# Biased attention and channel mix: float64 weights converted by bits, their range tested on a second read, low parts made by TensorE

## The chip, the core and the metric

The kernel runs on one core of one Trainium2 chip. The metric is the device time of one execution in microseconds. The engines are called as the profile calls them: PE (TensorE, matmuls) with PEld (its weight loads), DVE (VectorE), ACT (ScalarE), POOL (GpSimd) and SP (SyncE, which issues the DMAs).

## What is computed

An attention with a distance bias over a sliding window of 96 keys and 8 global keys, and behind it a channel mix with a gate. Shapes: q, k, v are (4, 8, 768, 64) in float32; w_k is (512, 1024), w_v (1024, 512) and w_r (512, 512), all three in float64.

```python
keep = (pos_k < 8) | ((rel >= 0) & (rel < 96))
scores = where(keep, q @ k.T / 8 - slope[h] * dist, -1e9)
x = softmax(scores) @ v                     # heads side by side: (4, 768, 512)
xk = mu_k * x + (1 - mu_k) * x_prev         # x_prev: the row before in the sequence
xr = mu_r * x + (1 - mu_r) * x_prev
k2 = relu(xk @ w_k) ** 2
out = sigmoid(xr @ w_r) * (k2 @ w_v)
```

## The kernel before

The sequence is cut into 24 tiles of 128 rows (6 for each of 4 batches). For each tile the attention makes scores on PE (`scores`, line 302), adds the bias on DVE (L323), takes the exponential on ACT (L324), scales by the reciprocal of the sum on POOL or ACT (L332 to L337), transposes on PE (L349), copies on ACT (L351) and multiplies with v on PE (L368). Tiles 0 to 7 multiply q and k as whole float32 (L314, L315); later tiles use split operands.

Two tiles make a chunk of 256 rows, and there are 12 chunks. `ffn` (L451) mixes each chunk with the row before it (`mix`, DVE L395) and splits it into a high and a low part (`xk_hi` by an ACT cast, `xk_lo` by a DVE subtraction). `channel_mix` (L400) multiplies them with split weights, three matmuls for each product (high x high, high x low, low x high: `three`, L403). In a chunk there are four blocks `kp` for xk @ w_k, each followed by Relu on ACT (L431), the square on DVE (L432), the high part on ACT (L433) and the low part on DVE (L434); then two blocks `z` for the gate, and two blocks `vps` for the product with w_v, each followed by the multiplication on DVE (L448) and the store. The three PSUM tiles of `ps_f` (tag "f") are shared by kp, z and vps.

The weights come as float64 and are converted in ten steps of 1 MB: w_k has steps 0 to 3, w_r has 4 and 5, w_v has 6 to 9. `weight_load` reads the two 32-bit words of each number (`low`, `top`). `weight_begin` (L161) builds a float32 `wa` from them: ACT takes an absolute value with a scale (L172 or L175), which clamps what is out of float32's range together with a POOL operation for w_k (L173) or a DVE operation for the others (L176); then DVE puts exponent, sign and fraction together with three bit operations (L177 to L179), and ACT casts the high part (L181). `weight_end` (L184) makes the low part by a DVE subtraction (L187).

A loop over tiles (L475) interleaves attention and channel mix by a budget, and the tables `W_LOADS` and `W_BEGUN` say when weight steps are loaded and begun. The order in which each engine then works is made by a scheduler at build time, from its own costs; each engine runs its list in order. At the end a flag `wide_i` is read by all five engines (L630), which then branch over a general path (`wide`) for sizes outside the tables (L631). The flag depends on the two sizes alone, and DVE writes it in the first 10 us.

Of the kernel before, what the change touches and what calls it, by code (L numbers as in the profile page):

```python
# [9 lines left out]
F32 = mybir.dt.float32  # L10
F32R = mybir.dt.float32r
# [30 lines left out]
def tile_biased_attention_channel_mix(ctx: ExitStack, tc: tile.TileContext, qT, kT, v, n_sizes, mu_kr, w_k, w_v, w_r, q_rows, k_rows, v_rows, slopes, out):  # L42
# [102 lines left out]
    pool.tensor_scalar(mus1, mus, -1.0, 1.0, op0=ALU.mult, op1=ALU.add)  # L145

    w_steps = [(name, src, j) for name, src, pairs in (("k", w_k, 4), ("r", w_r, 2), ("v", w_v, 4)) for j in range(pairs)]
    w_raw, w_live = {}, {}

    def weight_load(i):  # L150


        name, src, j = w_steps[i]
        raw = w_raw[i] = const.tile([128, 1024, 2], I32, tag=f"w{i}", name=f"w64_{i}")
        if name == "k":
            ins = nc.sync.dma_start(raw.rearrange("p n w -> p (n w)"), src[j * 128 : (j + 1) * 128, :])
        else:
            ins = nc.sync.dma_start(raw.rearrange("p (k n) w -> p k (n w)", k=2), src[j * 256 : (j + 1) * 256, :].rearrange("(k p) m -> p k m", p=128))
        tc.keep_in_program_order(ins)

    def weight_begin(i):  # L161


        name, src, j = w_steps[i]
        raw = w_raw.pop(i)
        a = p4k.tile([128, 1024], I32, tag="t4k", name=f"wa_{i}")
        low, top = raw[:, :, 0], raw[:, :, 1]

        if name == "k":
            act.activation(a.bitcast(F32), top.bitcast(F32), AF.Abs, scale=2.0**111)  # L172
            pool.tensor_scalar(a.bitcast(F32), a.bitcast(F32), 2.0**-112, 2.0**-111, op0=ALU.mult, op1=ALU.mult)  # L173
        else:
            act.activation(a.bitcast(F32), top.bitcast(F32), AF.Abs, scale=2.0**16)  # L175
            vec.tensor_scalar(a.bitcast(F32), a.bitcast(F32), 2.0, HUGE, op0=ALU.max, op1=ALU.min)  # L176
        vec.tensor_scalar(a, a, 3, 0x7FFFFFF8, op0=ALU.logical_shift_left, op1=ALU.bitwise_and)  # L177
        vec.scalar_tensor_tensor(a, top, -0x80000000, a, op0=ALU.bitwise_and, op1=ALU.bitwise_or)
        vec.scalar_tensor_tensor(a, low, 29, a, op0=ALU.logical_shift_right, op1=ALU.bitwise_or)  # L179
        both = const.tile([128, 2, 1024], F32R, tag=f"w{i}", name=f"w{name}{j}")  # L180
        act.copy(both[:, 0, :], a.bitcast(F32))  # L181
        w_live[i] = a, both

    def weight_end(i):  # L184
# [117 lines left out]
    def scores(n, hp):  # L302
        t = n % NT
        s = state[n]
        c0 = 0 if t else OWN
        w = W - c0
        p = pat if t else pat0
        ps = ps_s.tile([128, 512], F32, name=f"s_{n}_{hp}", tag="s")
        for u in range(2):
            h = 2 * hp + u  # L310
            o = ps[:, u * 256 : u * 256 + w]
            if n < NATIVE:
                if t:
# [12 lines left out]
        if hp % 2 == 0:  # L326
            return
        h0, nh = 2 * hp - 2, 4
        r = s_pool.tile([128, nh], F32, name=f"r_{n}_{hp}", tag="r", bufs=8)
        vec.tensor_scalar(r, s["sum"][:, h0 : h0 + nh], 1.0e-9, None, op0=ALU.add)  # L330
        vec.reciprocal(r, r)  # L331
        for u in range(nh):  # L332
            e = s["e"][h0 + u]
            if n < 6 and u < 2:
                act.mul(e[:, :w], e[:, :w], r[:, u : u + 1])
            else:
                pool.tensor_scalar(e[:, :w], e[:, :w], r[:, u : u + 1], 1.0, op0=ALU.mult, op1=ALU.mult)  # L337
# [59 lines left out]
        vec.tensor_sub(lo, tmp, hi)  # L397
        return hi, lo

    def channel_mix(xk, xr, out_rows, f_pool, f2_pool, ps_f):  # L400
        kkh, kkl = (part(f_pool, f"kk_{p}", 8) for p in ("hi", "lo"))

        def three(o, sh, sl, mh, ml, first, last):  # L403
            pe.matmul(o, sh, mh, start=first, stop=False)  # L404
            pe.matmul(o, sh, ml, start=False, stop=False)  # L405
            pe.matmul(o, sl, mh, start=False, stop=last)  # L406

        def z_of(i):
            z = ps_f.tile([128, 512], F32, name="z", tag="f")
            c = slice(i * 128, (i + 1) * 128)  # L410
            for k in range(4):
                three(z, xr[0][:, k, c], xr[1][:, k, c], *wts["r", k], k == 0, k == 3)
                yield
            sig = f2_pool.tile([128, 512], F32, name="sig", tag="f2")
            sigs.append((z, sig))

        sigs = []
        for fp in range(4):
            weights_need(4)
            ps = ps_f.tile([128, 512], F32, name="kp", tag="f")  # L420
# [12 lines left out]
            act.copy(kkh[:, 2 * fp : 2 * fp + 2, :], kk)  # L433
            vec.tensor_sub(kkl[:, 2 * fp : 2 * fp + 2, :], kk, kkh[:, 2 * fp : 2 * fp + 2, :])  # L434
        weights_need(6)
        for i in range(2):
            yield from z_of(i)
        for z, sig in sigs:
            act.activation(sig, z, AF.Sigmoid)
        for i in range(2):  # L440
            c = slice(i * 128, (i + 1) * 128)
            vp = ps_f.tile([128, 512], F32, name="vps", tag="f")
            sig = sigs[i][1]
            for f in range(8):
# [12 lines left out]

    LAG = 3
# [218 lines left out]
```

## Time and profile before

| what | value |
|---|---|
| time, median of 3 runs | 511.14 us (510.61 to 512.39) |
| the profiled execution | 510.47 us, of which the span of the trace is 508.6 us |
| PE busy in the span | 490.6 us (96%) |
| DVE, ACT, POOL busy | 345.8, 338.0 and 215.7 us |
| moved by DMA | 49.46 MB, mean 97 GB/s |

The span runs from the first to the last instruction of the program; the execution's own time is 1.9 us longer. A busy share says how much of the span an engine had an instruction in work, and the granted clock says at which of its two levels TensorE ran (1.00 is 2.4 GHz, 0.50 is 1.2 GHz). The shares are means over stretches that differ, so the stretches are read apart below.

### The profile page before, as it was taken

How to read it: one execution, taken by the hardware profiler on the slowest of the kernel's cores; microseconds unless marked ns; L12 is line 12 of the kernel's file. 1: busy time of each engine (PE TensorE's matmuls, PEld its weight loads, DVE VectorE, ACT ScalarE, POOL GpSimd, SP SyncE). 2: the span in 40 equal slices, each digit the busy share in tenths (PEclk: the TensorE clock that was granted, in tenths of full speed). 3: DMA queues.
4: the chain of work that ended last, by engine and by line, in shares of the span. 5: the costliest groups of instructions: out<-in, count | busy, mean ns of one | idle time of the engine just before them, and what ended most of it. 6: DMA issues, size and time to landing. Idle time of an engine off the chain costs nothing. (4 is left out here: it accounts for less than half of the span.)

```text
span 508.6 us, 10113 instructions
## 1 busy us (share of the span) xinstructions
PE 490.6 (96%) x3562; PEld 434.5 (85%) x3562; DVE 345.8 (68%) x826; ACT 338.0 (66%) x826; POOL 215.7 (42%) x359
## 2 busy tenths in 40 slices
PE   7949998999999999999999999999999999999996
PEld 4838987998898898898898898898898898898984
DVE  6799989755468777757768767757768765535321
ACT  4999999757448759567668578567668578654230
POOL 7432216243348546427538436527538535203000
PEclk9987999999999999999999999999999999999999
DMA  8998611513733333433323433333433221100101
GB/s 236 320 245 233 214 43 39 121 43 79 172 92 79 104 101 81 107 97 80 105 84 79 105 101 79 104 101 79 106 82 80 64 60 39 41 1 2 41 2 46
DMA packets 21353, 49.46 MB, mean 97 GB/s; under 512 B 5008, under 2 KB 6032, under 8 KB 20784
## 3 DMA queue, kind: packets, MB, share of 16 engines
q1 hardware_dynamic: 21152, 48.74, 35.4%
q8 instruction: 30, 0.49, 0.4%
q14 instruction: 27, 0.22, 0.1%
q10 hardware_dynamic: 144, 0.00, 0.0%
HBM read 42.44 MB, written 6.29 MB: 96 GB/s over the span
## 5 line engine op out<-in xcount | busy, mean ns | idle before, releaser
L337 POOL TENSOR_SCALAR e<-e,r 128x232 f32<-128x232 f32 (+1 forms) x168 | 82.4, 507 | 162.1 <-DVE r L331 134.1
L404 PE MATMUL kp<-xk_hi,wk 128*128 128x256 f32 x384 | 108.4, 283 | 0.4 <-ACT xk_hi L396 0.4
L405 PE MATMUL kp<-xk_lo,wk 128*128 128x256 f32 x384 | 107.3, 280 | 0.0
L406 PE MATMUL kp<-xk_hi,wk 128*128 128x256 f32 x384 | 107.2, 279 | 0.0
L324 ACT ACTIVATE e<-e,nmax 128x232 f32<-128x232 f32 (+1 forms) x192 | 89.6, 470 | 22.9 <-DVE nmax L323 22.3
L323 DVE CUSTOM_DVE_ANT_0 e<-s,pat 128x232 f32<-128x232 f32 (+1 forms) x192 | 64.5, 373 | 24.8 <-PE s L318 14.3
L404 PE MATMUL vps<-wv,kk_hi 128*128 128x512 f32 x192 | 75.2, 394 | 0.0
L406 PE MATMUL vps<-wv,kk_lo 128*128 128x512 f32 x192 | 75.2, 392 | 0.0
L405 PE MATMUL vps<-wv,kk_hi 128*128 128x512 f32 x192 | 75.2, 391 | 0.0
L404 PEld LDWEIGHTS kp<-xk_hi,wk 128*128 128x128 f32 x384 | 72.0, 188 | 1.4 <-ACT xk_hi L396 0.6
L405 PEld LDWEIGHTS kp<-xk_lo,wk 128*128 128x128 f32 x384 | 72.1, 188 | 0.4
L406 PEld LDWEIGHTS kp<-xk_hi,wk 128*128 128x128 f32 x384 | 72.1, 188 | 0.0
L432 DVE TENSOR_TENSOR kk<-kp,kk 128x512 f32<-128x512 f32 x48 | 33.1, 689 | 46.5 <-ACT kk L431 46.3
L351 ACT COPY et<-t 128x256 f32<-128x256 f32 (+1 forms) x176 | 56.2, 372 | 8.6 <-PE t L349 8.0
L349 PE MATMUL t<-ident,e 128*128 128x128 f32 x352 | 55.8, 281 | 0.1
L349 PEld LDWEIGHTS t<-ident,e 128*128 128x128 f32 x352 | 41.4, 138 | 8.7 <-issue 0.5
L368 PE MATMUL av<-et,va 128*64 128x128 f32 x384 | 42.3, 285 | 5.0 <-ACT et L351 5.0
L434 DVE TENSOR_TENSOR kk_lo<-kk,kk_hi 128x512 fp32r<-128x512 f32 x48 | 34.5, 721 | 17.1 <-ACT kk_hi L433 16.7
L431 ACT ACTIVATE kk<-kp 128x512 f32<-128x512 f32 x48 | 28.3, 590 | 24.6 <-PE kp L406 24.4
L433 ACT CAST kk_hi<-kk 128x512 fp32r<-128x512 f32 x48 | 29.8, 623 | 21.0 <-DVE kk L432 20.2
L406 PEld LDWEIGHTS vps<-wv,kk_lo 128*128 128x128 f32 x192 | 36.0, 188 | 7.7
L405 PEld LDWEIGHTS vps<-wv,kk_hi 128*128 128x128 f32 x192 | 36.2, 188 | 6.8
(101 smaller groups left out, 1070.6 us busy)
## 6 DMA issues: line engine op xcount, KB each, us to landing
qraw<-in_qT_dram SPq DMA_DIRECT2D x32, 256.0 KB
kraw<-in_kT_dram SPq DMA_DIRECT2D x32, 256.0 KB
out_dram<-sig SPq DMA_DIRECT2D x24, 256.0 KB
va<-in_v_dram SPq DMA_DIRECT2D x20, 240.0 KB
vb<-in_v_dram SPq DMA_DIRECT2D x20, 208.0 KB
w<-in_w_k_dram SPq DMA_DIRECT2D x4, 1024.0 KB
w<-in_w_v_dram SPq DMA_DIRECT2D x4, 1024.0 KB
qz<-in_qT_dram SPq DMA_DIRECT2D x8, 256.0 KB
```

The lines of the kernel that those rows point to most:

```text
L323: vec.tensor_tensor_reduce(out=e[:, :w], in0=o, in1=p[:, h, :], op0=ALU.add, op1=ALU.min, scale=-0.125, scalar=3.0e38, accum_out=s["nmax"] ...
L324: act.activation(e[:, :w], e[:, :w], AF.Exp, bias=s["nmax"][:, h : h + 1], scale=-1.0, accum_out=s["sum"][:, h : h + 1])
L337: pool.tensor_scalar(e[:, :w], e[:, :w], r[:, u : u + 1], 1.0, op0=ALU.mult, op1=ALU.mult)
L349: pe.transpose(pt[0:p, c : c + 128], e[:, k * 128 : k * 128 + p], ident)
L351: act.copy(et[0:p, k * 256 : k * 256 + 256], pt[0:p, k * 256 : k * 256 + 256])
L368: pe.matmul(o, vt[:, h * 64 : (h + 1) * 64], et[0:p, c + q : c + 128], start=k == 0, stop=k == nb - 1)
L404: pe.matmul(o, sh, mh, start=first, stop=False)
L405: pe.matmul(o, sh, ml, start=False, stop=False)
L406: pe.matmul(o, sl, mh, start=False, stop=last)
L432: vec.tensor_mul(kk, pv, kk)
L433: act.copy(kkh[:, 2 * fp : 2 * fp + 2, :], kk)
L434: vec.tensor_sub(kkl[:, 2 * fp : 2 * fp + 2, :], kk, kkh[:, 2 * fp : 2 * fp + 2, :])
```

## The change

Four things change.

1. The absolute value and the clamps are gone. The first bit operation reads `top` from the loaded words, with other masks: a number whose exponent lies in float32's range comes out as before.
2. What is out of that range is found late: all weights are read a second time, in 20 loads of 512 KB (`range_load`), into buffers of the attention that are free by then. For each load DVE takes four exponent bits, and ACT sums their distance from 7.5 (`range_test`). Loads and tests are called behind each kp block of chunks 10 and 11. At the end the sums are reduced (`worst`, one small matmul `row`), and the flag `wide_i` takes the result in. The general path converts the weights anew (`weights_any`).
3. The low parts of w_k and w_r (steps 0 to 5) are made on PE, in halves of 512 columns: the identity times `wa` plus minus the identity times the high part, added up in a PSUM tile `rest` of `ps_f`, and copied out by ACT. w_v keeps the subtraction on DVE.
4. In tiles 0 to 5, ACT scales one head of each four, and POOL three; it was two and two.

```diff
     make_identity(nc, ident)
+    minus = const.tile([128, 128], F32R, name="minus")
+    nc.scalar.mul(minus, ident, -1.0)
...
-        if name == "k":
-            act.activation(a.bitcast(F32), top.bitcast(F32), AF.Abs, scale=2.0**111)
-            pool.tensor_scalar(a.bitcast(F32), a.bitcast(F32), 2.0**-112, 2.0**-111, op0=ALU.mult, op1=ALU.mult)
-        else:
-            act.activation(a.bitcast(F32), top.bitcast(F32), AF.Abs, scale=2.0**16)
-            vec.tensor_scalar(a.bitcast(F32), a.bitcast(F32), 2.0, HUGE, op0=ALU.max, op1=ALU.min)
-        vec.tensor_scalar(a, a, 3, 0x7FFFFFF8, op0=ALU.logical_shift_left, op1=ALU.bitwise_and)
-        vec.scalar_tensor_tensor(a, top, -0x80000000, a, op0=ALU.bitwise_and, op1=ALU.bitwise_or)
+        vec.tensor_scalar(a, top, 3, 0x3FFFFFF8, op0=ALU.logical_shift_left, op1=ALU.bitwise_and)
+        vec.scalar_tensor_tensor(a, top, -0x40000000, a, op0=ALU.bitwise_and, op1=ALU.bitwise_or)
         vec.scalar_tensor_tensor(a, low, 29, a, op0=ALU.logical_shift_right, op1=ALU.bitwise_or)
...
-        vec.tensor_sub(both[:, 1, :], a.bitcast(F32), both[:, 0, :])
+        if name in 'kr':
+            for o in (0, 512):
+                rest = ps_f.tile([128, 512], F32, name=f"rest_{i}_{o}", tag="f")
+                pe.matmul(rest, ident, a.bitcast(F32)[:, o : o + 512], start=True, stop=False)
+                pe.matmul(rest, minus, both[:, 0, o : o + 512], start=False, stop=True)
+                act.copy(both[:, 1, o : o + 512], rest)
+        else:
+            vec.tensor_sub(both[:, 1, :], a.bitcast(F32), both[:, 0, :])
...
+    def range_load():
+        n = len(words_again)
+        if n == 20:
+            return
+        name, src, j = w_steps[n // 2]
+        if n % 2:
+            raw = p4k.tile([128, 512, 2], I32, tag="t4k", name=f"again_{n}")
+        else:
+            raw = q_pool.tile([128, 512, 2], I32, tag=("qh", "ql")[n // 2 % 2], name=f"again_{n}")
...
+        nc.sync.dma_start(raw.rearrange("p n w -> p (n w)"), src[at * 128 : (at + 1) * 128, o : o + 1024])
+        words_again.append(raw)
+
+    def range_test(behind_vec, behind_act):
...
+        with tc.issue_after(behind_vec.ins):
+            vec.tensor_scalar(low, top, 27, 15, op0=ALU.logical_shift_right, op1=ALU.bitwise_and)
+        with tc.issue_after(behind_act.ins):
+            act.activation(top.bitcast(F32), low, AF.Abs, bias=middle, accum_out=odd[:, n : n + 1])
...
-            if n < 6 and u < 2:
+            if n < 6 and u < 1:
                 act.mul(e[:, :w], e[:, :w], r[:, u : u + 1])
...
+            high = act.copy(kkh[:, 2 * fp : 2 * fp + 2, :], kk)
+            rest = vec.tensor_sub(kkl[:, 2 * fp : 2 * fp + 2, :], kk, kkh[:, 2 * fp : 2 * fp + 2, :])
+            if more:
+                for i in range(3):
+                    range_load()
+                for i in range(3):
+                    range_test(rest, high)
...
+    worst = const.tile([128, 2], F32, name="worst")
+    vec.reduce_max(worst[:, 0:1], odd, axis=AX.X)
+    row = ps_f.tile([128, 512], F32, name="row", tag="f")
+    pe.matmul(row[0:1, 0:128], worst[:, 0:1], ident, start=True, stop=True)
+    vec.reduce_max(worst[0:1, 1:2], row[0:1, 0:128], axis=AX.X)
     fast.close()
...
     vec.tensor_scalar(okf[:, 0:1], okf[:, 0:1], -1.0, 1.0, op0=ALU.mult, op1=ALU.add)
+    vec.scalar_tensor_tensor(okf[0:1, 0:1], worst[0:1, 1:2], 256.0, okf[0:1, 0:1], op0=ALU.is_gt, op1=ALU.max)
     vec.tensor_copy(wide_i, okf[0:1, 0:1])
```

The change moves instructions. First PE, early in the program, where the last products with v of tile 0 (`av`) stand ahead of scores (`s`). Before:

```order
L368 MATMUL av_378<-et_2_326,va_189 64x128 x2
L368 MATMUL av_378<-et_3_353,va_189 64x128 x2
L314 MATMUL s_2_461<-kz_177,qz_172 128x104
L315 MATMUL s_2_461<-kz_180,qz_172 128x128
L314 MATMUL s_2_461<-kz_177,qz_172 128x104
L315 MATMUL s_2_461<-kz_180,qz_172 128x128
```

Now, at the same place:

```order
L404 MATMUL av_396<-et_2_339,va_194 64x128 x2
L404 MATMUL av_396<-et_3_371,va_194 64x128 x2
L188 MATMUL rest_0_249<-wa_210,ident 128x512
L188 MATMUL rest_512_253<-wa_210,ident 128x512
L350 MATMUL s_0_421<-kz_182,qz_177 128x104
L189 MATMUL rest_0_249<-wk_214,minus 128x512
L189 MATMUL rest_512_253<-wk_214,minus 128x512
```

Four matmuls for the first weight step have come in; all 24 of the six steps stand ahead of the first kp.

Second DVE, in the four kp blocks of the last chunk (the square of a block, then its low part). Before:

```order
L432 TENSOR_TENSOR kk<-kp,kk 128x512
L434 TENSOR_TENSOR kk_lo<-kk,kk_hi 128x512
L432 TENSOR_TENSOR kk<-kp,kk 128x512
L434 TENSOR_TENSOR kk_lo<-kk,kk_hi 128x512
L432 TENSOR_TENSOR kk<-kp,kk 128x512
```

Now:

```order
L468 TENSOR_TENSOR kk<-kp,kk 128x512
L470 TENSOR_TENSOR kk_lo<-kk,kk_hi 128x512
L220 TENSOR_SCALAR again_5916<-again_5916 128x512
L220 TENSOR_SCALAR again_5918<-again_5918 128x512
L220 TENSOR_SCALAR again_5920<-again_5920 128x512
L468 TENSOR_TENSOR kk<-kp,kk 128x512
L470 TENSOR_TENSOR kk_lo<-kk,kk_hi 128x512
L220 TENSOR_SCALAR again_5958<-again_5958 128x512
```

Between the low part of one block and the square of the next stand three tests, each of which waits for its load. ACT's list holds three tests between its blocks as well.

Third DVE at the end of the program (the last two multiplications with the gate). Before:

```order
L432 TENSOR_TENSOR kk<-kp,kk 128x512
L434 TENSOR_TENSOR kk_lo<-kk,kk_hi 128x512
L448 TENSOR_TENSOR sig<-vps,sig 128x512 x2
L630 TENSOR_LOAD wide_i
L631 COMPARE_AND_BRANCH
```

Now:

```order
L554 TENSOR_REDUCE worst<-odd 128x1
L489 TENSOR_TENSOR sig<-vps,sig 128x512 x2
L557 TENSOR_REDUCE worst<-row 1x1
L692 SCALAR_TENSOR_TENSOR okf<-worst,okf 1x1
L693 CAST wide_i<-okf 1x1
L695 TENSOR_LOAD wide_i
L696 COMPARE_AND_BRANCH
```

The flag is now written behind the last multiplication, and every engine's branch waits for it.

## Rows read from the trace of the kernel before

**Rows 1.** The page, part 1: busy us, share of the span, instructions.

```profile
PE 490.6 (96%) x3562; PEld 434.5 (85%) x3562; DVE 345.8 (68%) x826; ACT 338.0 (66%) x826; POOL 215.7 (42%) x359
```

**Rows 2.** Windows: stretch, length, busy us of each engine, PEclk, DMA share, GB/s.

```profile
17.00:24.00 7.00, 6.19 (x57) 5.18 (x56) 6.93 (x21) 7.00 (x22) 3.26 (x4) 1.00 1.03 360
24.00:33.60 9.60, 5.32 (x49) 4.18 (x48) 8.72 (x21) 9.60 (x27) 3.31 (x5) 1.00 1.04 275
33.60:43.80 10.20, 7.80 (x45) 7.50 (x43) 10.20 (x19) 9.10 (x23) 4.64 (x5) 0.50 0.99 226
43.80:48.50 4.70, 4.30 (x37) 3.20 (x36) 4.70 (x14) 3.68 (x9) 0.33 (x1) 0.99 0.59 234
80.00:90.00 10.00, 8.65 (x69) 6.64 (x68) 8.35 (x19) 9.97 (x27) 5.29 (x8) 1.00 0.00 1
90.00:440.00 350.00, 349.85 (x2598) 313.51 (x2599) 244.42 (x580) 238.24 (x586) 171.41 (x282) 1.00 0.34 88
440.00:503.60 63.60, 63.55 (x429) 56.39 (x427) 21.99 (x36) 20.94 (x41) 7.21 (x14) 1.00 0.06 20
```

**Rows 3.** Timeline of PE, 24 to 49 us: rows behind idle time [idle, releaser].

```profile
26.44 0.43 PE L368 MATMUL av<-et,va 128*64 128x128 f32 x2 [1.18 <-ACT et L351]
...
33.17 0.43 PE L368 MATMUL av<-et,va 128*64 128x128 f32 x2 [2.45 <-ACT et L351]
...
37.48 0.72 PE L314 MATMUL s<-kz,qz 128*128 128x104 f32 x2 [2.40 <-DMA qz<-in_qT_dram]
...
48.48 0.62 PE L404 MATMUL kp<-xk_hi,wk 128*128 128x256 f32 x3 [0.40 <-ACT xk_hi L396]
```

**Rows 4.** Timeline of PE at full clock (start, duration): float32 scores; the last vps.

```profile
77.83 0.41 PE L315 MATMUL s<-kz,qz 128*128 128x128 f32 x2
78.07 0.37 PE L314 MATMUL s<-kz,qz 128*128 128x104 f32 x2
78.27 0.41 PE L315 MATMUL s<-kz,qz 128*128 128x128 f32 x2
...
497.72 0.39 PE L406 MATMUL vps<-wv,kk_lo 128*128 128x512 f32 x1
...
503.16 0.39 PE L406 MATMUL vps<-wv,kk_lo 128*128 128x512 f32 x1
```

**Rows 5.** Groups of DVE by form: count, busy us, mean ns, idle before.

```profile
L178 DVE SCALAR_TENSOR_TENSOR wa<-w,wa 128x1024 int32<-128x1024 int32 x10 | 12.4, 1242 | 0.0
...
L177 DVE TENSOR_SCALAR wa<-wa 128x1024 int32<-128x1024 int32 x10 | 6.8, 681 | 0.9 <-POOL wa L173 0.9
L187 DVE TENSOR_TENSOR wk<-wa,wk 128x1024 fp32r<-128x1024 f32 x4 | 5.8, 1444 | 0.0
```

**Rows 6.** Groups of ACT by form, the same columns.

```profile
L431 ACT ACTIVATE kk<-kp 128x512 f32<-128x512 f32 x48 | 28.3, 590 | 24.6 <-PE kp L406 24.4
...
L172 ACT ACTIVATE wa<-w 128x1024 f32<-128x1024 f32 x4 | 4.6, 1152 | 0.0
```

**Rows 7.** Timelines of ACT and PE: the last chunk's last high part, its first vps.

```profile
488.58 0.62 ACT L433 CAST kk_hi<-kk 128x512 fp32r<-128x512 f32 x1 [0.76 <-DVE kk L432]
...
492.51 0.39 PE L404 MATMUL vps<-wv,kk_hi 128*128 128x512 f32 x1
```

**Rows 8.** The end: DVE's last work; flag load, branch, first instruction behind (ns; us).

```profile
503.66 0.69 DVE L448 TENSOR_TENSOR sig<-vps,sig 128x512 f32<-128x512 f32 x1 [4.75 <-PEq L631]
...
L630 DVEq TENSOR_LOAD <-wide_i x1: 543/543/543, 503.7 to 503.7; - x1
...
L631 POOLq COMPARE_BRANCH  x1: 45/45/45, 465.0 to 465.0; - x1
L631 POOLq EVENT_SEMAPHORE  x1: 17/17/17, 468.9 to 468.9; - x1
...
L631 DVEq EVENT_SEMAPHORE  x1: 21/21/21, 507.3 to 507.3; - x1
...
L673 SPq EVENT_SEMAPHORE  x10: 17/28/28, 507.3 to 508.6; - x10
```

More of the change, by code (lines that the diff above doesn't have):

```diff
@@ L147, in tile_biased_attention_channel_mix, with weight_words @@
     w_steps = [(name, src, j) for name, src, pairs in (("k", w_k, 4), ("r", w_r, 2), ("v", w_v, 4)) for j in range(pairs)]
-    w_raw, w_live = {}, {}
+    w_raw, w_live, w_done = {}, {}, {}
+    def weight_words(i, raw):
+        name, src, j = w_steps[i]
+        if name == "k":
+            return nc.sync.dma_start(raw.rearrange("p n w -> p (n w)"), src[j * 128 : (j + 1) * 128, :])
+        return nc.sync.dma_start(raw.rearrange("p (k n) w -> p k (n w)", k=2), src[j * 256 : (j + 1) * 256, :].rearrange("(k p) m -> p k m", p=128))
     def weight_load(i):
-        name, src, j = w_steps[i]
         raw = w_raw[i] = const.tile([128, 1024, 2], I32, tag=f"w{i}", name=f"w64_{i}")
-        if name == "k":
-            ins = nc.sync.dma_start(raw.rearrange("p n w -> p (n w)"), src[j * 128 : (j + 1) * 128, :])
-        else:
-            ins = nc.sync.dma_start(raw.rearrange("p (k n) w -> p k (n w)", k=2), src[j * 256 : (j + 1) * 256, :].rearrange("(k p) m -> p k m", p=128))
-        tc.keep_in_program_order(ins)
+        tc.keep_in_program_order(weight_words(i, raw))
     def weight_begin(i):
@@ L167, in weight_begin @@
         low, top = raw[:, :, 0], raw[:, :, 1]
-        if name == "k":
-            act.activation(a.bitcast(F32), top.bitcast(F32), AF.Abs, scale=2.0**111)
-            pool.tensor_scalar(a.bitcast(F32), a.bitcast(F32), 2.0**-112, 2.0**-111, op0=ALU.mult, op1=ALU.mult)
-        else:
-            act.activation(a.bitcast(F32), top.bitcast(F32), AF.Abs, scale=2.0**16)
-            vec.tensor_scalar(a.bitcast(F32), a.bitcast(F32), 2.0, HUGE, op0=ALU.max, op1=ALU.min)
-        vec.tensor_scalar(a, a, 3, 0x7FFFFFF8, op0=ALU.logical_shift_left, op1=ALU.bitwise_and)
-        vec.scalar_tensor_tensor(a, top, -0x80000000, a, op0=ALU.bitwise_and, op1=ALU.bitwise_or)
+        vec.tensor_scalar(a, top, 3, 0x3FFFFFF8, op0=ALU.logical_shift_left, op1=ALU.bitwise_and)
+        vec.scalar_tensor_tensor(a, top, -0x40000000, a, op0=ALU.bitwise_and, op1=ALU.bitwise_or)
         vec.scalar_tensor_tensor(a, low, 29, a, op0=ALU.logical_shift_right, op1=ALU.bitwise_or)
@@ L182, in weight_begin @@
         w_live[i] = a, both
+        w_done[i] = both
     def weight_end(i):
@@ L190, in weight_end @@
             wts[name, j if name == "k" else 2 * j + k] = kn[:, 0, :], kn[:, 1, :]
+    words_again, tested = [], [0]
+    def range_load():
[7 more added lines that the diff above has]
+            raw = q_pool.tile([128, 512, 2], I32, tag=("qh", "ql")[n // 2 % 2], name=f"again_{n}")
+        at, o = divmod((j * 2 + n % 2) * 512 // 512 * 1024 + n % 1 * 1024, 2048 if name == "k" else 1024)
+        nc.sync.dma_start(raw.rearrange("p n w -> p (n w)"), src[at * 128 : (at + 1) * 128, o : o + 1024])
+        words_again.append(raw)
+    def range_test(behind_vec, behind_act):
+        n = tested[0]
+        if n == len(words_again):
+            return
+        tested[0] += 1
+        raw = words_again[n]
+        low, top = raw[:, :, 0], raw[:, :, 1]
+        with tc.issue_after(behind_vec.ins):
+            vec.tensor_scalar(low, top, 27, 15, op0=ALU.logical_shift_right, op1=ALU.bitwise_and)
+        with tc.issue_after(behind_act.ins):
+            act.activation(top.bitcast(F32), low, AF.Abs, bias=middle, accum_out=odd[:, n : n + 1])
+    odd = const.tile([128, 20], F32, name="odd")
+    middle = const.tile([128, 1], F32, name="middle")
+    pool.memset(middle, -7.5)
     w_count = [0, 0, 0]
@@ L398, in mix, with channel_mix @@
         return hi, lo
-    def channel_mix(xk, xr, out_rows, f_pool, f2_pool, ps_f):
+    def channel_mix(xk, xr, out_rows, f_pool, f2_pool, ps_f, more=False):
         kkh, kkl = (part(f_pool, f"kk_{p}", 8) for p in ("hi", "lo"))
@@ L432, in channel_mix @@
             vec.tensor_mul(kk, pv, kk)
-            act.copy(kkh[:, 2 * fp : 2 * fp + 2, :], kk)
-            vec.tensor_sub(kkl[:, 2 * fp : 2 * fp + 2, :], kk, kkh[:, 2 * fp : 2 * fp + 2, :])
+            high = act.copy(kkh[:, 2 * fp : 2 * fp + 2, :], kk)
[5 more added lines that the diff above has]
+                    range_test(rest, high)
         weights_need(6)
@@ L454, in ffn @@
         xr = mix(xt[:, :, 1:257], xt[:, :, 0:256], "r", p4k, f_pool, c == 0)
-        return channel_mix(xk, xr, lambda i: out[(2 * c + i) * 128 : (2 * c + i + 1) * 128, :], f_pool, f2_pool, ps_f)
+        return channel_mix(xk, xr, lambda i: out[(2 * c + i) * 128 : (2 * c + i + 1) * 128, :], f_pool, f2_pool, ps_f, c >= 10)
     LAG = 3
@@ L510, in tile_biased_attention_channel_mix, with weights_any @@
         run_ffn(1.0)
-    fast.close()
+    assert tested[0] == 20
+    worst = const.tile([128, 2], F32, name="worst")
[3 more added lines that the diff above has]
+    vec.reduce_max(worst[0:1, 1:2], row[0:1, 0:128], axis=AX.X)
+    fast.close()
+    def weights_any():
+        with ExitStack() as g:
+            work = g.enter_context(tc.tile_pool(name="g_words", bufs=1))
+            for i, both in w_done.items():
+                raw = work.tile([128, 1024, 2], I32, name="g_raw", tag="g_raw")
+                a = work.tile([128, 1024], I32, name="g_a", tag="g_a")
+                weight_words(i, raw)
+                low, top = raw[:, :, 0], raw[:, :, 1]
+                act.activation(a.bitcast(F32), top.bitcast(F32), AF.Abs, scale=2.0**16)
+                vec.tensor_scalar(a.bitcast(F32), a.bitcast(F32), 2.0, HUGE, op0=ALU.max, op1=ALU.min)
+                vec.tensor_scalar(a, a, 3, 0x7FFFFFF8, op0=ALU.logical_shift_left, op1=ALU.bitwise_and)
+                vec.scalar_tensor_tensor(a, top, -0x80000000, a, op0=ALU.bitwise_and, op1=ALU.bitwise_or)
+                vec.scalar_tensor_tensor(a, low, 29, a, op0=ALU.logical_shift_right, op1=ALU.bitwise_or)
+                act.copy(both[:, 0, :], a.bitcast(F32))
+                vec.tensor_sub(both[:, 1, :], a.bitcast(F32), both[:, 0, :])
     def wide():
+        weights_any()
         with ExitStack() as g:
```

## The prediction

> **What bounds the kernel now.** I read the page's busy shares first: PE works 96% of the span [rows 1]. A mean over stages says little, so I read the stretches next. From 90 us to the last matmul PE is busy 349.85 of 350 and 63.55 of 63.6 us at full clock [rows 2]: there, nothing that DVE, ACT or POOL save moves the end. What PE loses, it loses early. Between 17.0 and 48.5 us it is busy 6.19 + 5.32 + 7.80 + 4.30 = 23.61 of 31.5 us, so 7.9 us are idle; another 1.35 us are idle between 80 and 90 us. And from 33.6 to 43.8 us, after the stretch with most idle time, the granted clock is 0.50, the lower level, so half of the 7.80 busy us (3.9) are lost as well. All that an earlier or better filled start can give back is 7.9 + 1.35 + 3.9 = 13.1 us.
>
> Then I read whom PE waited for [rows 3]: twice for ACT's copies of transposes (1.18 and 2.45 us), once for a load of q (2.40 us), and for xk_hi just before the first kp at 48.48 us. ACT and DVE are the reason behind most of it: from 24 to 43.8 us ACT is busy 18.7 of 19.8 us and DVE 18.9. The weight conversion is a large part of their work, and the change takes on just that. The question is what it costs on PE, the engine that sets the end.
>
> **The change, part by part.**
>
> *Low parts on PE.* Six steps by two halves by two matmuls make 24 new matmuls of 512 columns, all ahead of the first kp. Those of the high part are of the kind of vps: 24 starts from 497.72 to 503.16 us, 0.227 us each [rows 4]; 12 of them cost 2.7 us. Those with the identity multiply whole float32, of which the trace has scores only: 0.24 us from start to start with 128 columns and 0.20 us with 104 [rows 4]. On by that slope, 512 columns take 0.24 + 384 x 0.04 / 24 = 0.88 us; four times the price of 128 gives 0.96. I take 0.90, near the slope, since a part of each short matmul is fixed. Twelve cost 10.8 us. Together PE gets 13.5 us more (13.3 to 14.2), at full clock.
>
> *What DVE, ACT and POOL get back.* Ahead of xk_lo, DVE loses four subtractions of w_k (L187, 1.44 us) and one first bit operation, but the scheduler puts four more of the other bit operations there (1.24 us) [rows 5]: 4 x 1.44 + 0.68 - 4 x 1.24 = 1.5 us. That holds if the first bit operation keeps its 0.68 us though it now reads every other word. No row here shows a DVE operation with one input and such steps; bounds are 0.68 and, by L178 which reads the same words with a second input, 1.24, which would make 8 x 0.56 = 4.5 us. I take 0.68, the same operation. The Trainium skill speaks for that too (VectorE: DVE Perf Modes, "Mode 2×_2P — use both read ports for one tensor"): a one-input operation on SBUF runs at two elements per cycle, and the conditions it lists don't include a step of one. ACT loses seven absolute values ahead of xk_hi (1.15 us each) and gets nine copies of rest, the nearest row being Relu from PSUM (0.59 us) [rows 6]: 8.1 - 5.3 = 2.8 us less. POOL is idle most of that time (busy 3.26 + 3.31 + 4.64 + 0.33 = 11.5 of 31.5 us [rows 2]), so the scaling that it takes on is hidden there; and ACT, which gives it up, saves less per operation than the 0.59 us of Relu's 512 columns, since a scaling has 232 at most. I count neither.
>
> *How much of the 13.5 us the gaps take.* Without any gap between 17.0 us and the first kp, PE has 23.61 - 3.9 = 19.7 us of old work at full clock and 13.5 us of new; so the first kp can't start before 17.0 + 33.2 = 50.2 us, against 48.48. PE is now what is late there, not ACT. The gaps will not be filled wholly: a rest waits for DVE's last bit operation, then for ACT's high cast, its PSUM tile for ACT's copy, and behind it on PE, in order, stand the scores that DVE waits for; both engines stay near full. I take the lower clock as gone (3.9 us), since PE has work in the stretch ahead of it, and two thirds of the idle time, 2/3 x 9.2 = 6.2 us: 10.1 of 13.1 us come back. Bounds: all of it, or a third of the idle time and no clock (3.1 us).
>
> *Second read and tests.* 20 x 512 KB are 10.5 MB in a stretch that moves 20 GB/s at a DMA share of 0.06, while 349 to 360 GB/s passed early on [rows 2]: 10.5 MB would take some 30 us at that rate, and the two chunks last 60. In the last chunk a test is some 0.34 to 0.62 us of DVE (half of L177 or L178 [rows 5]) and 0.58 to 1.15 us of ACT (half or the whole of L172 [rows 6]), eight tests each. They stand in order between a block's low part and the next block's square, so kp's PSUM tiles and kk_hi and kk_lo wait behind them. The cover: kk_hi of the last block is done at 489.2 us, and the first vps, which needs the first blocks only, starts at 492.51 [rows 7]; it comes to the last block's parts 18 matmuls (4.1 us) later. In 63.6 us ACT and DVE are busy 21 and 22 us [rows 2]. So I cost the tests at nothing. Without cover they would cost at most ACT's 8 x 1.15 = 9.2 us less those 7.4.
>
> *The end.* Now POOL branches already at 465.0, and it took 3.9 us from its branch to the first instruction behind it (468.9); DVE branches behind its last multiplication and took 2.95 us from that one's end (504.35) to 507.3 [rows 8]. POOL's jump lies under other work. With the change the flag is written behind the last multiplication (ends 504.35): a reduction, a combination and a cast, all on a few numbers. No row prices these; each costs between nothing and the 0.69 us of that multiplication's 512 columns [rows 8], and I take 0.2, in the lower part, since their columns are few: about 504.95; 0.54 us to load the flag, and then POOL's 3.9 us: 509.4, against 507.3 now. The 1.3 us from there to the end stay. That is 2.1 us more; if only DVE's own path counts, 1.2. The Trainium skill has a rule on this (Runtime: NRT & Kernel Launch, "Instruction fetch mechanics"): a taken branch to a target outside the instructions at hand must fetch them first. The trace agrees, with POOL's 3.9 us.
>
> **The sum.** 13.5 - 10.1 + 2.1 = +5.5 us, on the profiled execution's 510.47: 516.0. The median of the runs is 0.67 us higher, 511.14, and from there it is 516.6. I predict 516.5.
>
> **Rivals.**
>
> *The gaps take nearly all.* For it: rest matmuls are independent of the attention and many. Against it: they hang on the two busiest engines. 13.5 - 13.1 + 2.1 = +2.5: 513.6.
>
> *The start gets worse.* PE stops in order behind rest matmuls, the lower clock stays and the strided bit operation is slow. For it: ACT and DVE at 0.9 and more, three PSUM tiles. 13.5 - 3.1 + 2.1 = +12.5: 523.6.
>
> *A test holds the tail.* A load comes late, DVE stops ahead of a square, and PE runs out of PSUM tiles. For it: buffers are freed by earlier tests, so loads follow tests closely. Against it: the cover above. Two late loads at the longest DMA wait that PE has now (2.40 us [rows 3]) add 4.8: 521.
>
> *The other side: float32 with 512 columns is cheap.* If the identity matmuls took the 0.227 us of the others, PE would get 5.4 us and the sum is 5.4 - 10.1 + 2.1 = -2.6: 508.5. It turns at a price of (10.1 - 2.1) / 12 = 0.67 us for a pair. The scores' 0.24 us for 128 columns speak against it.
>
> *The change doesn't do what it says:* the test sends the program to the general path, which computes all again, far outside this range.
>
> **Chances.** The forecast (514.5 to 519) 0.50, gaps take nearly all 0.20, worse start 0.17, tail 0.08, cheap float32 0.04, general path 0.01. About 0.3% (1.5 us) is what a measurement of this kernel can tell from no change. Cheap float32 is faster: 0.04. Within 0.3% needs +1.5 or less: full filling and the lower bounds of price and end together (13.3 - 13.1 + 1.2 = +1.4), 0.07 of the second case. Slower: 0.89. The range begins at that +1.4, 512.5, and takes most of the worse start and the tail in, up to 522.5.
>
> **What would show it.** First kp at 52 to 54 us; identity matmuls near 0.9 us from start to start; granted clock 1.00 from 33.6 to 43.8 us; PE busy all the time in chunks 10 and 11; POOL's first instruction behind the branch some 2 us later against the last multiplication than DVE's now. It would be wrong if the identity matmuls cost well under 0.67 us, if PE still idles 8 us ahead of the first kp, or if PE waits between 450 us and the last vps.

## The result, and the profile after

The changed kernel takes 517.2 us (median of four executions; three of them took 516.18 to 517.73, the fourth was disturbed and stays out of the ratio), the kernel before 510.9. The ratio is 1.0111, with a 95% interval of 1.0079 to 1.0144: slower by some 5.7 us, where 516.5 us were forecast. The sum is met, its terms are not: the experiments show that the start gained where I took a loss, that the end cost more than I took, and that the largest single loss is in a place that the prediction does not name. The profiled execution is the one of 517.73 us, with a span of 516.0.

The page of the changed kernel, part 1, answers to [rows 1]:

```profile
PE 503.1 (98%) x3600; PEld 438.4 (85%) x3600; DVE 344.8 (67%) x837; ACT 345.8 (67%) x857; POOL 220.4 (43%) x368
```

The windows of the same kernel answer to [rows 2] (stretch, length, busy us of PE, PEld, DVE, ACT and POOL, granted clock, DMA share, GB/s):

```profile
17.00:24.00 7.00, 7.00 (x44) 4.67 (x45) 5.54 (x16) 6.14 (x20) 1.99 (x2) 0.89 1.01 359
24.00:33.60 9.60, 9.60 (x64) 7.14 (x64) 9.46 (x27) 9.48 (x29) 6.29 (x7) 1.00 1.02 279
33.60:43.80 10.20, 10.20 (x71) 7.07 (x68) 9.15 (x21) 9.04 (x19) 5.18 (x7) 1.00 0.73 204
43.80:48.50 4.70, 4.70 (x30) 3.03 (x31) 2.37 (x6) 4.70 (x17) 0.63 (x1) 1.00 0.90 315
80.00:90.00 10.00, 10.00 (x60) 8.52 (x59) 9.77 (x19) 9.93 (x22) 3.35 (x6) 1.00 0.17 47
90.00:440.00 350.00, 349.99 (x2608) 312.81 (x2607) 239.12 (x569) 236.03 (x580) 169.18 (x281) 1.00 0.35 93
440.00:507.60 67.60, 67.60 (x441) 58.99 (x439) 30.00 (x64) 36.69 (x87) 8.70 (x16) 1.00 0.43 144
```

From 17.0 to 48.5 us PE is busy all the time, where it was idle for 7.9 us, and the granted clock from 33.6 to 43.8 us is 1.00, where it was 0.50. The lower clock has not vanished, it stands earlier: 0.50 from 8.6 to 18.5 us, and the 0.89 of the first row holds the end of it (e2 and e3 take this up). The 1.35 us of 80 to 90 us are gone. In chunks 10 and 11, DVE and ACT work 30 and 37 us in place of 22 and 21, and PE waits for none of it. Read alone, this says that the start went better than forecast.

The rest matmuls in the timeline of PE (start, duration, what; the row behind each shows when PE went on) answer to the scores of [rows 4]:

```profile
37.99 1.12 PE L188 MATMUL rest<-wa,ident 128*128 128x512 f32 x2
38.95 0.36 PE L350 MATMUL s<-kz,qz 128*128 128x104 f32 x2
...
41.20 1.02 PE L188 MATMUL rest<-wa,ident 128*128 128x512 f32 x2
42.06 1.04 PE L385 MATMUL t<-ident,e 128*128 128x128 f32 x8
42.86 0.48 PE L189 MATMUL rest<-wr,minus 128*128 128x512 f32 x1
43.17 0.36 PE L350 MATMUL s<-kz,qz 128*128 128x104 f32 x2
...
44.06 1.02 PE L188 MATMUL rest<-wa,ident 128*128 128x512 f32 x2
44.52 0.79 PE L189 MATMUL rest<-wr,minus 128*128 128x512 f32 x1
45.16 0.36 PE L350 MATMUL s<-kz,qz 128*128 128x104 f32 x2
```

An identity matmul holds PE for 0.96 us (37.99 to 38.95) or 0.86 (41.20 to 42.06), one with minus for 0.31, a pair for 1.10 (44.06 to 45.16). The forecast was 0.90 and 0.227.

The last vps matmuls answer to the second part of [rows 4]:

```profile
501.82 0.40 PE L442 MATMUL vps<-wv,kk_lo 128*128 128x512 f32 x1
...
507.42 0.40 PE L442 MATMUL vps<-wv,kk_lo 128*128 128x512 f32 x1
```

These are again 24 starts apart: 5.60 us, so 0.233 us each. Before it was 5.44 us, 0.227. This is the line to stop at. Shape, operands and neighbours are the same, PE is never idle in either kernel, the clock is 1.00 in both, and from start to start each matmul takes 3% longer. A busy share cannot show it.

The end, in the timeline and in the rows of the flag's load and branch (for the latter: count, duration in ns, start of first and last), answers to [rows 8]:

```profile
507.93 0.69 DVE L489 TENSOR_TENSOR sig<-vps,sig 128x512 f32<-128x512 f32 x1 [4.98 <-PE vps L442]
508.54 0.27 DVE L557 TENSOR_REDUCE worst<-row 1x1 f32<-1x128 f32 x1
508.84 0.15 DVE L692 SCALAR_TENSOR_TENSOR okf<-worst,okf 1x1 f32<-1x1 f32 x1
509.02 0.14 DVE L693 CAST wide_i<-okf 1x1 int32<-1x1 f32 x1
```

```profile
L695 DVEq TENSOR_LOAD <-wide_i x1: 839/839/839, 509.2 to 509.2; - x1
...
L696 ACTq COMPARE_BRANCH  x1: 45/45/45, 510.0 to 510.0; - x1
L696 POOLq COMPARE_BRANCH  x1: 45/45/45, 510.1 to 510.1; - x1
L696 PEldq COMPARE_BRANCH  x1: 3578/3578/3578, 510.1 to 510.1; - x1
L696 DVEq COMPARE_BRANCH  x1: 72/72/72, 510.1 to 510.1; - x1
...
L696 POOLq EVENT_SEMAPHORE  x1: 17/17/17, 510.5 to 510.5; - x1
...
L696 PEldq EVENT_SEMAPHORE  x1: 51/51/51, 513.7 to 513.7; - x1
L696 DVEq EVENT_SEMAPHORE  x1: 21/21/21, 514.2 to 514.2; - x1
...
L738 SPq EVENT_SEMAPHORE  x10: 17/28/28, 514.6 to 515.9; - x10
```

From the end of the last multiplication (508.62) to the end of the span it takes 7.4 us; it was 508.6 - 504.35 = 4.25. So of the 7.4 us between the two spans (516.0 and 508.6) 3.1 lie behind the last multiplication, and 4.3 ahead of it. The reduction, combination and cast are over at 509.16, DVE's load at 510.0, and PE and DVE come out of the branch at 513.7 and 514.2. ACT and POOL need 0.5 us for it.

A table of all that PE did helps to tell these pieces apart. I summed the timeline of PE from 17 us on, giving each row the time from its start to the start of the next, so that a wait counts to the row ahead of it (the trace of e6 is of its slowest execution, 519.49 us, so its first column is not compared):

| kernel | av + s + t | rest | kp | z | vps |
|---|---|---|---|---|---|
| before | 145.4 | | 138.7 | 67.8 | 134.1 |
| changed | 130.7 | 14.3 | 141.0 | 69.0 | 135.2 |
| e1: low parts on DVE | 143.1 | | 141.1 | 69.1 | 135.4 |
| e3: no tests, early flag | 130.1 | 14.3 | 139.2 | 67.8 | 132.4 |
| e6: before, one pool moved | 147.9 | | 141.4 | 68.8 | 136.5 |
| e9: flag in odd | 128.6 | 15.1 | 140.3 | 68.1 | 132.7 |

### The profile page after: what moved, and what is told of

It reads as the page before. It is cut to its first block, busy times and chain, and to the rows that moved or that the text cites. A ratio compares the mean times of both kernels' runs of the same rounds, so it can differ in the third digit from the quotient of the medians.

```text
span 516.0 us, 10305 instructions
## 1 busy us (share of the span) xinstructions
PE 503.1 (98%) x3600; PEld 438.4 (85%) x3600; DVE 344.8 (67%) x837; ACT 345.8 (67%) x857; POOL 220.4 (43%) x368
## 4 chain that ended last, share of the span: by engine, by line
PE 96%; DVE 1%; DMA 1%; issue 0%; POOL 0%; DVEq 0%; POOLq 0%
PE kp L440 9%; PE kp L442 9%; PE kp L441 9%; PE vps L440 9%; PE vps L442 9%; PE vps L441 9%; PE av L404 8%; PE t L385 8%; PE z L440 4%; PE z L441 4%; PE z L442 4%; PE s L351 3%; PE s L354 3%; PE s L353 3%; PE s L350 2%; PE rest L188 2%
## 5 line engine op out<-in xcount | busy, mean ns | idle before, releaser
L373 POOL TENSOR_SCALAR e<-e,r 128x232 f32<-128x232 f32 (+1 forms) x180 | 90.4, 520 | 162.4 <-DVE r L367 134.6
L440 PE MATMUL kp<-xk_hi,wk 128*128 128x256 f32 x384 | 109.6, 285 | 0.0
L442 PE MATMUL kp<-xk_hi,wk 128*128 128x256 f32 x384 | 108.5, 283 | 0.0
L440 PE MATMUL vps<-wv,kk_hi 128*128 128x512 f32 x192 | 76.3, 398 | 0.0
L441 PE MATMUL vps<-wv,kk_hi 128*128 128x512 f32 x192 | 76.0, 396 | 0.0
L470 DVE TENSOR_TENSOR kk_lo<-kk,kk_hi 128x512 fp32r<-128x512 f32 x48 | 35.6, 741 | 22.8 <-ACT kk_hi L469 22.4
L440 PEld LDWEIGHTS vps<-wv,kk_hi 128*128 128x128 f32 x192 | 36.2, 189 | 7.3
L441 PEld LDWEIGHTS vps<-wv,kk_hi 128*128 128x128 f32 x192 | 36.2, 188 | 7.3
L415 ACT COPY x<-av 128x512 f32<-128x512 f32 x24 | 14.1, 587 | 41.0 <-PE av L404 40.9
```

Of the source, the lines that this page charges most:

```text
L470: rest = vec.tensor_sub(kkl[:, 2 * fp : 2 * fp + 2, :], kk, kkh[:, 2 * fp : 2 * fp + 2, :])
```

## The experiments

The ratios are to the kernel before on the same chip, with 95% intervals. "Places" are the addresses that a built program gives its tiles: `const` stands first, the pools behind it, so a new small tile in `const` moves every pool behind it (in steps of 32 bytes). `minus` and `odd` stand ahead of the weights and move weights and pools alike; `worst` stands behind the weights, so it moves the pools and the weights stay.

**e1: the low parts of w_k and w_r by DVE again** (the tile `minus` goes too).

```diff
-        if name in 'kr':
...
-        else:
-            vec.tensor_sub(both[:, 1, :], a.bitcast(F32), both[:, 0, :])
+        vec.tensor_sub(both[:, 1, :], a.bitcast(F32), both[:, 0, :])
```

> The changed kernel with the low parts of w_k and w_r subtracted on DVE again; bit conversion, tests and late flag stay. Theory A (PE is full from 17 us on, the new matmuls are paid in full and only filled gaps come back): PE gets some 13.8 us less and idles again before the first kp, but less than before, since ACT has lost its absolute values. Gaps as large as before (13.1 us with the lower clock) would give 516.5, gaps a third smaller 512; I expect 512 to 515 us, idle time of PE from 17 to 50 us of 4 us or more, and still 7 us from the last sig to the end. Rival C (it is the lower clock from 8.6 to 18.5 us that costs): the same time as the changed kernel, 516 to 517.5. Rival D (DVE's subtractions were what was late): slower than the changed kernel.

Measured: 517.4 us, ratio 1.0127 (1.0104 to 1.0151), the same as with PE's low parts. My expectation, 512 to 515, fell; rival C is answered with e2 and e3. Rows of PE with the idle time ahead of them and what ended it:

```profile
20.64 0.47 PE L341 MATMUL s<-kz,qz 128*128 128x104 f32 x2 [0.75 <-POOL kz L239]
...
24.16 0.44 PE L376 MATMUL t<-ident,e 128*128 128x128 f32 x2 [1.02 <-POOL e L364]
...
37.08 0.73 PE L341 MATMUL s<-kz,qz 128*128 128x104 f32 x2 [5.45 <-DMA qz<-in_qT_dram]
```

PE waits again, now for a load of q (5.45 us) and for POOL (L364 is the scaling, of which part 4 gives POOL more); the table has 143.1 us on the attention's rows in place of 130.7. So 12.4 of the 14.3 us of rest matmuls go into time that PE otherwise waits.

**e2 and e3: the flag early; then no tests either.** In e2 the lines from `worst = ...` to the second `reduce_max` go, and:

```diff
-    vec.scalar_tensor_tensor(okf[0:1, 0:1], worst[0:1, 1:2], 256.0, okf[0:1, 0:1], op0=ALU.is_gt, op1=ALU.max)
```

In e3 the calls of `range_load` and `range_test` go as well.

> The changed kernel with second read and tests, but without the reduction of their sums and without it in the flag, so that the flag is written at about 10 us as before; what is left out is that a bad weight is acted on. Theory A: only the end changes, from 7.4 us behind the last sig to 4.3: 3.1 us less than the changed kernel, 513 to 514. Rival B (the second read and the tests cost, not the branch): within 0.7 us of the changed kernel.

> The changed kernel without second read, tests and late flag; what is left out is the range test of the weights. Theory A: the same as the one with tests and an early flag, within 0.7 us (513 to 514), since PE is busy all through chunks 10 and 11 either way. Rival B: 2 us or more below that one.

Measured: e2 510.0 us, ratio 0.9970 (0.9952 to 0.9988); e3 508.7, ratio 0.9953 (0.9938 to 0.9968). Both are faster than the kernel before. The tests cost 0.2%, which the intervals do not tell from nothing (the two medians, from one chip, are 1.3 us apart). The early flag brings twice what the end explains, 1.4% against 3.1 us (0.6%). The timeline of e2 has the rest of it in the vps rows:

```profile
495.62 0.39 PE L442 MATMUL vps<-wv,kk_lo 128*128 128x512 f32 x1
...
501.06 0.39 PE L442 MATMUL vps<-wv,kk_lo 128*128 128x512 f32 x1
```

That is 5.44 us for 24, the 0.227 us of before. PE's list of instructions is the same as in the changed kernel up to `row`. So either an open flag slows PE, or the tile `worst`, which e2 and e3 do not have, does it by its place.

e2 and e3 also answer rival C of the expectations. From 8.6 to 18.5 us e3 has the lower clock, as the changed kernel has, and e2 has not (windows of e2, then of e3):

```profile
8.60:18.50 9.90, 8.88 (x44) 7.13 (x43) 7.83 (x37) 7.25 (x31) 5.24 (x11) 1.00 1.05 334
```

```profile
8.60:18.50 9.90, 8.36 (x36) 6.89 (x36) 7.83 (x37) 6.95 (x29) 5.06 (x11) 0.50 1.05 335
```

Yet PE worked at one pace in both at first. In e2, at a recorded 1.00, two matmuls of the scores (128 and 104 columns) took 0.85 us (timeline of PE):

```profile
12.58 0.68 PE L351 MATMUL s<-kz,qz 128*128 128x128 f32 x2
...
13.43 0.68 PE L351 MATMUL s<-kz,qz 128*128 128x128 f32 x2
```

In e3, at 0.50, the same two took 0.85 as well (12.72 to 13.57 us), against 0.44 in [rows 4]. The first kp starts at 51.5 us in e2 and at 52.3 in e3, the last vps at 501.06 and 501.3. So that stretch does not explain a loss of 5.7 us.

**e4: each rest pair twice.**

```diff
+                for again in range(2):
-                pe.matmul(rest, ident, ...)
-                pe.matmul(rest, minus, ...)
+                    pe.matmul(rest, ident, ...)
+                    pe.matmul(rest, minus, ...)
```

> The changed kernel with each pair of rest matmuls done twice, the second pair overwriting the first. Theory A: PE has no idle time left, so the second 24 matmuls are paid in full: 12 times 1.1 to 1.2 us, 13 to 14.5 us above the changed kernel, 530 to 532. Rival C: PE still has room, 0 to 7 us above. An identity matmul as cheap as the one with minus would give 5.4 us above.

Measured: 527.7 us, ratio 1.0326 (1.0301 to 1.0351), 11.0 us above the changed kernel, between theory A's 13 to 14.5 and rival C's 7, nearer to theory A. The first set had found room; the second, which holds PE for 12.4 us (the sum of the rest rows rises from 14.3 to 26.7), pays 11 of them. PE had hardly any waits left for it.

**e5, e6 and e7: places.** e5 makes `worst` 64 bytes wide in the changed kernel. e6 and e7 take the kernel before; no instruction moves in any of them.

```diff
-    worst = const.tile([128, 2], F32, name="worst")
+    worst = const.tile([128, 16], F32, name="worst")
```
```diff
-    f_pool.tile([128, 96], F32, name="ahead", tag="ahead")
+    f_pool.tile([128, 104], F32, name="ahead", tag="ahead")
```
```diff
+    const.tile([128, 8], F32, name="front")
     sizes_w = const.tile([128, 2, 2], I32, name="sizes_w")
```

> The changed kernel, all of it, with the tile worst made 64 bytes wide in place of 8, so that every tile behind it stands 32 bytes further; no instruction moves. Theory P (the late flag costs twice: 2.4 to 3.1 us behind the last sig, and some 4 us because the small tile worst moves the tiles of the channel mix to addresses from which PE's matmuls start 0.233 instead of 0.227 to 0.230 us apart): as with the early flag (510.0) plus the end, 512 to 513.5, vps at 0.227 to 0.230. Rival F (a flag that is still open slows PE itself, wherever the tiles are): as the changed kernel, 516 to 517.5, vps at 0.233.

> The kernel before, with an unused tile at the front of the pool of xk, xr and kk made 32 bytes wider; only this pool and the one behind it (kk, sig) move, by 32 bytes, and no instruction does. Theory P: kp, z and vps take 2 to 2.5% longer, some 5 to 6 us: 516 to 517.5. Rival F: no change, 510.5 to 511.5.

> The kernel before, with an unused tile of 32 bytes at the very front, so that weights, ident and every other tile move by 32 bytes together. If it is how weights and xk or kk stand to each other: no change, 510.5 to 511.5. If it is where xk and kk stand in themselves: 516 to 517.5, as when they alone move. Rival F: no change; this run alone does not tell F from the first.

Measured: e6 515.7 us, ratio 1.0092 (1.0068 to 1.0117); e7 509.9, 0.9989 (0.9972 to 1.0005); e5 516.3, 1.0097 (1.0069 to 1.0126), its vps 0.233 us apart. The kernel before, with nothing but 32 unused bytes ahead of xk, xr and kk, loses almost what the change loses, and its last vps are again 0.233 us apart:

```profile
506.44 0.40 PE L406 MATMUL vps<-wv,kk_lo 128*128 128x512 f32 x1
...
512.04 0.40 PE L406 MATMUL vps<-wv,kk_lo 128*128 128x512 f32 x1
```

With everything moved together nothing is lost. So it is the distance between the two operands of a matmul that counts (xk or kk against the weights), not where they stand in themselves. Theory P holds for e6, but not with the 64 bytes of e5, which left open whether F is true besides.

**e9: worst in unused columns of odd.** `odd` takes 96 bytes with 20 columns and with 24, so the distance is that of the kernel before, and all of the change is computed.

```diff
-    odd = const.tile([128, 20], F32, name="odd")
+    odd = const.tile([128, 24], F32, name="odd")
...
-    worst = const.tile([128, 2], F32, name="worst")
...
```

What used `worst` uses columns 20 and 21 of `odd`.

> The changed kernel, all of it, with the two numbers of the tile worst kept in unused columns of the tile odd, so that the tiles of the channel mix stand to the weights as in the kernel before; the late flag stays. Theory P (the place slows kp, z and vps, and 64 bytes were as bad as 32): as the kernel with the early flag, plus the end: 512 to 513.5, vps 0.227 to 0.230 us apart, still 7 us from the last sig to the end. Rival F (the open flag slows PE): 516 to 517.5, vps 0.233 us apart.

Measured: 512.2 us, ratio 1.0036 (1.0020 to 1.0053). The vps are back at 0.227 us with the flag as late as ever, and the end is as long as in the changed kernel (502.83 to 510.2, 7.4 us):

```profile
496.20 0.39 PE L442 MATMUL vps<-wv,kk_lo 128*128 128x512 f32 x1
...
501.64 0.39 PE L442 MATMUL vps<-wv,kk_lo 128*128 128x512 f32 x1
```

Its end, in the timeline and in the rows of branch and last semaphores:

```profile
502.14 0.69 DVE L489 TENSOR_TENSOR sig<-vps,sig 128x512 f32<-128x512 f32 x1 [4.82 <-PE vps L442]
```

```profile
L695 DVEq EVENT_SEMAPHORE  x1: 21/21/21, 508.6 to 508.6; - x1
...
L737 SPq EVENT_SEMAPHORE  x10: 17/28/28, 508.9 to 510.1; - x10
```

That refutes F. The interval lies below that of the changed kernel: 0.75% (3.8 us) of the changed kernel's time is the place.

**e11 and e12: the pool of xk, xr and kk moved by 128 and 256 bytes** (`ahead` with 128 and 160 columns in the kernel before).

> The kernel before with the pool of xk, xr and kk moved by 128 bytes. If the place counts in steps of 128 bytes: no change, 510 to 511. If in larger steps: kp, z and vps are slower as with 32 bytes, 514 to 516.

> The kernel before with the pool of xk, xr and kk moved by 256 bytes. Steps of 128 or 256 bytes: no change, 510 to 511. Larger steps: 514 to 516.

Measured: 510.3 us, 0.9995 (0.9983 to 1.0007), and 510.6, 1.0002 (0.9992 to 1.0011). The time of e11 looks like no effect, but its rows show two that cancel (the last kp matmuls, 12 starts apart, and the last vps, 24):

```profile
484.82 0.28 PE L406 MATMUL kp<-xk_hi,wk 128*128 128x256 f32 x1
...
486.18 0.28 PE L406 MATMUL kp<-xk_hi,wk 128*128 128x256 f32 x1
...
497.20 0.40 PE L406 MATMUL vps<-wv,kk_lo 128*128 128x512 f32 x1
...
502.79 0.40 PE L406 MATMUL vps<-wv,kk_lo 128*128 128x512 f32 x1
```

```profile
485.46 0.28 PE L406 MATMUL kp<-xk_hi,wk 128*128 128x256 f32 x1
...
486.88 0.28 PE L406 MATMUL kp<-xk_hi,wk 128*128 128x256 f32 x1
...
497.68 0.39 PE L406 MATMUL vps<-wv,kk_lo 128*128 128x512 f32 x1
...
503.12 0.39 PE L406 MATMUL vps<-wv,kk_lo 128*128 128x512 f32 x1
```

With 128 bytes a kp comes every 0.113 us instead of 0.118 (e12), and a vps every 0.233 instead of 0.227. With 256 both are as before. The step of 128 bytes that I expected is wrong for each of them alone.

**e8: bits alone** (e3 with DVE's subtractions; the edits of e1 and e3 together).

> The conversion by bits alone, with DVE's subtractions, without second read, tests and late flag, ACT scaling one head fewer as in the change; what is left out is the range test. xk and kk stand as in the kernel before, 128 bytes on. The one with PE's low parts instead, otherwise the same, took 508.7. Theory A as on record (PE pays for the rest matmuls what the gaps don't take, net 3.4 us): 505 to 507. Rival G (the rest matmuls find room that DVE's subtractions would have left empty; their 14.3 us and the refilled time cancel): 508 to 510. Rival D (DVE is what is late, so the subtractions cost more than the matmuls): above 510.

Measured: 508.4 us, ratio 0.9955 (0.9937 to 0.9974); e3, with PE's low parts, has 0.9953. Rival G holds: bits, with the scaling of part 4, bring all that there is, 2.3 us, and part 3 adds nothing that can be told from noise.

**e10: five tests behind a block**, so that all lie in chunk 10 and the reduction is called in chunk 11.

```diff
-                for i in range(3):
+                for i in range(5):
...
```

The same edit in the loop of `range_test`; `worst` stays in `odd` as in e9, and the lines of the reduction move to the calls of chunk 11.

> The same, with five loads and tests behind each block in place of three, so that all twenty lie in chunk 10 and the flag can be written in chunk 11; all of the change is still computed. Theory P: the branches of ACT and POOL lie under PE's work again and the end is that of the kernel before (4.3 us behind the last sig): 509.5 to 511, 2.5 us below the one with the late flag. Rival B (tests that stand closer hold up chunk 10, PE waits there): 512 or more, with idle time of PE between 445 and 480 us.

Measured: 511.5 us, ratio 1.0024 (1.0007 to 1.0041), not told from e9's, and between theory P's 509.5 to 511 and rival B's 512. The end is short again (the last multiplication ends at 509.41 us and the span at 513.9, 4.5 us later), but in the profile part of it is lost in chunk 11, as rival B said (windows; then the row of PE that waits, and the row of POOL behind that):

```profile
475.00:480.00 5.00, 3.27 (x18) 2.38 (x17) 4.18 (x9) 2.56 (x5) 3.23 (x4) 1.00 0.00 0
480.00:485.00 5.00, 5.00 (x30) 4.50 (x30) 2.60 (x6) 1.64 (x2) 0.00 (x0) 0.66 0.13 52
```

```profile
479.16 0.39 PE L441 MATMUL kp<-xk_lo,wk 128*128 128x256 f32 x1 [1.74 <-DVE xk_lo L433]
```

```profile
472.22 2.27 POOL L430 TENSOR_SCALAR mix_k<-x,mus 128x256 f32<-128x256 f32 x4 [27.15 <-DMA again<-in_w_v_dram]
```

Mixing chunk 11 waits for a buffer of the second read; PE waits 1.74 us for xk_lo, and the granted clock of the stretch behind it is 0.66. This profile is of the slowest of 12 executions (515.64 us), so the size is its own. No version that acts on the range test beats the kernel before.

## Why the prediction was right, and where it was not

The parts, from the ratios at 511 us: conversion, low parts on PE and scaling together -2.4 us (e3), second read and tests +0.9 (e2 against e3, not told from nothing), late flag +3.4 (e9 against e2; the traces have 7.4 and 4.8 us at the end, 2.6 apart), place of `worst` +3.8 (the changed kernel against e9). Each compares one kernel with the next, so that they add up to the measured 5.7 by construction. The forecast had +3.4 for the start, 0 for the tests and +2.1 for the end.

- *Low parts on PE.* The price was right: 14.3 us against 13.5 (13.3 to 14.2), and 0.86 to 0.96 us for an identity matmul on a slope from 128 columns.
- *How much the gaps take* is the step that failed. I took 10.1 of at most 13.1 us back. The attention's rows got 145.4 - 130.7 = 14.7 us shorter, more than the whole price of the rest matmuls, and the bound itself was too low. It was made of idle time and the lower clock, and a PE row counts as busy for 0.37 to 0.41 us while the next can start after 0.20 to 0.24 [rows 4]: a wait of less than the difference is in no idle time. That this makes up the rest of the bound is argued, not measured. That nearly everything came back is shown by e1 and e8, which take as long without the rest matmuls as the changed kernel and e3 with them. Why is read from the waits of e1: PE waited not for DVE and ACT alone, which the rest matmuls hang on, but for POOL and for a load of q, which they do not (in e8 the profile puts the longest wait, 4.75 us on the same row, down to DVE instead). POOL's scaling, which the prediction counts as hidden, is among these waits; in the changed kernel, where PE has the rest matmuls to do, none is left.
- *First kp.* It started at 52.4 us, inside the forecast's 52 to 54, and would have passed for a proof. It is none: e3 has it at 52.3 us and ends 2 us before the kernel before, and e1 has it at 42.2 us and ends with the changed kernel. Work that moves ahead of a mark is not lost behind it.
- *DVE and ACT.* The strided bit operation took 0.69 us (0.68 taken), copies of rest 0.59 to 0.60 (medians). By the Trainium skill (VectorE: DVE Perf Modes, "Mode 2×_2P — use both read ports for one tensor") a one-input operation on SBUF has two results per cycle, and a step of one is not among the conditions; this trace agrees with its 0.69.
- *Tests.* DVE's took 0.43 us and ACT's 0.78 and 0.20, PE was busy for 67.60 of 67.6 us in these chunks, and the intervals leave 0 beside the 0.9.
- *The end.* Mechanism right, size low: 3.1 us in the trace for 2.1. The load took 0.84 us (0.54), the branch 4.1 (3.9), and the steps behind it 1.8 (1.3). The engine was wrong: POOL's branch, whose 3.9 us carried the term, took 0.5; PE's and DVE's took 3.6 and 4.1. The Trainium skill (Runtime: NRT & Kernel Launch, "Instruction fetch mechanics") has a taken branch to a target outside the instructions at hand wait for them to be fetched; the 3.6 and 4.1 agree with it, and the 0.5 of ACT and POOL in the same branch is not explained by it. Two slips of the prediction change little: DVE's own path alone adds 0.6 + 0.54 = 1.1 us, not 1.2, and the 349 GB/s are those of 8.6 to 17.0 us, which [rows 2] does not show.
- *Place.* No step of the prediction looked at it. The range test needs eight bytes for its result, and at 3.8 us they cost nearly as much as the reading, testing and branching that they serve (0.9 + 3.4). That the sum still came out is chance: 5.8 us missed at the start (3.4 forecast, -2.4 measured), and 3.8 + 1.3 + 0.9 found elsewhere.

## What to carry to other kernels

When PE is busy in both kernels and the time differs, compare the distance from start to start of one kind of matmul, late in the program; if that moved, look at what the edit did to the places of tiles before blaming its instructions, and test it with unused bytes. Work given to the busiest engine is free as far as that engine waits there for others, and waits shorter than a row's modelled duration are in no idle time. A flag that is known late shows its whole branch at the end, so a test should deliver its answer while there is still work to lie under.

## What the runs showed of the hardware that was not expected

Here the distance in SBUF between the two operands of a matmul sets how fast matmuls follow each other. Against the kernel before, vps (512 columns) came every 0.227 us at 0 and 256 bytes and every 0.233 at 32, 64 (e5) and 128; kp (256 columns) every 0.118 at 0 and 256, and 0.113 at 128. Kernels in which only the place differs show it (e6, e11, e12), and e7 shows that a common move does nothing. What lies behind it stays open. e11 suggests a version with xk 128 bytes on and kk where it is, which would have both of the better rates (some 3 us on kp); it was not tried.

In e2 and e3 the clock recorded from 8.6 to 18.5 us is 1.00 and 0.50, but around 13 us two matmuls of the scores took 0.85 us in both, against 0.44 in [rows 4]. So in that stretch the record alone did not tell how fast PE worked; why stays open.
